# Which DRAM run each SBUF partition takes: K and V pieces read in an interleaved order

## The chip, the cores and the metric

The kernel runs on one core of one Trainium2 chip. The metric is device time in microseconds (us) of one execution. The time before is 656.44 us, the median of three executions (656.38 to 656.63).

## What is computed

One decode step of a transformer block for a single token: layer norm, grouped-query attention over a cached context of 65,536 tokens, a residual, a second layer norm, a gated MLP and a second residual. All inputs are bf16.

```python
# x (1,1,512); k_cache, v_cache (1,8,65536,128); wq (512,4096); wo (4096,512)
q = layernorm(x) @ wq                      # 32 query heads of 128, four to each of the 8 KV heads
p = softmax(q . k_cache * 128**-0.5)       # over the 65,536 cached tokens
h = x + (p . v_cache) @ wo
g, u = layernorm(h) @ w_gate, layernorm(h) @ w_up      # 512 -> 1792
out = h + (sigmoid(g) * u) @ w_down
```

The two caches are 134 MB each; all weights together are some 14 MB. A softmax over tokens and the sum over V don't depend on the order in which the tokens are visited, as long as K and V use the same order.

## The kernel before, in words

**Pieces.** The work goes head by head, `h` = 0 to 7. The 65,536 tokens of a head of K, and of V, come in two *pieces* of 32,768 tokens, 8 MiB each (`PIECES`, line 229). A piece is spread over the 128 SBUF partitions: partition p holds 256 consecutive tokens, that is one DRAM *run* of 256 x 128 bf16 = 64 KiB. Within a partition a piece is 16 *chunks* of 16 tokens (`TC`), 4 KiB each. So a piece is 128 runs of 64 KiB, one for each partition, and the piece is contiguous in DRAM.

**The ring.** K and V pieces land in one SBUF tile, `ring`, with room for 36 chunks (line 230). `AT` (line 231) says where: the two K pieces of a head at chunks 0 and 4 (they overlap), both V pieces at chunk 20. Only the first head's K and the last head's V get two places apart, 0 and 20.

**Loads.** `load` (lines 325 to 331) issues one DMA for one piece, or for some columns (`cols`) of one. All are issued on SP's queue, in the order of the program: two loads of `wq`; K of head 0 in four parts of 8 chunks (lines 336 to 339); then for each head h = 1 to 7 the four pieces K h.0, V h-1.0, K h.1, V h-1.1 (lines 340 to 344); V 7.0; most of `wo`; V 7.1 in two parts (10 and 6 chunks, `LAST`); the rest of `wo`; and the weights of the MLP (lines 345 to 367). Each issue waits on SP until its place in the ring is free: a K piece waits for a mark F on VectorE, set when 12 of the 16 chunks of the K piece before it have been transposed (lines 526 to 528; `ORDER`, line 232, visits chunks 4 to 15 of the first piece first, so that the overlapping next piece can come in). A V piece waits for the matmuls that read the V piece before it (PV, line 599). SP does nothing else.

**Compute.** VectorE transposes each chunk of K in 32 x 32 blocks into `ktw` (line 525), TensorE forms the scores of four query heads from it (`pe_scores`, line 536; all matmuls with register addresses are recorded at line 436), VectorE and ScalarE form the softmax of the head (line 554), VectorE transposes the probabilities into `PT_sb` (line 581), and TensorE sums V with them (`pv`, line 599) while the next head's K comes in. The last head's sum is followed by `wo`, the second layer norm and the MLP (lines 822 to 880).

**What the step of the change touches.** Line 329 cuts the DRAM side of a piece into 128 rows, one for each partition; line 331 issues the DMA with that and the ring's columns. Every K and V load goes through these two lines: 18 of K and 17 of V. The weights have lines of their own.

Of the kernel before, what the change touches and what calls it, by code (L numbers as in the profile page):

```python
# [20 lines left out]
TC = 16  # L21
# [14 lines left out]
class Prog:  # L36
# [20 lines left out]
    def dma(self, eng, fn, sem, deps=(), name=None):  # L57
        self.op(eng, fn, deps, name)
        rec = self.dma_sems.setdefault(sem, dict(sem=None, count=0))
        rec["count"] += 16  # L60
        self.ops[eng][-1]["dma"] = (sem, rec["count"])
# [155 lines left out]
def bass_sequential_preLN__gqa_block_cached__glu_gated_glu__decode_kernel(  # L217
# [10 lines left out]
    CH = TC * DH  # L228
# [11 lines left out]
    with ExitStack() as es:  # L240
        def sb(name, shape, dt):
            return es.enter_context(nc.sbuf_tensor(name, shape, dt))
# [14 lines left out]
        ring = sb("ring", [128, RING], bf16)  # L257
# [57 lines left out]
        op, dma = P.op, P.dma  # L315
# [6 lines left out]
        def first_chunk(k, h, q):  # L322
            return AT[{("K", 0): "K0", ("V", HKV - 1): "V7"}.get((k, h), k)][q]

        def load(k, h, q, deps, sem, name, cols=None):
            j0, j1 = PIECES[q]
            a, z = cols or (j0, j1)
            cache = A_k_cache if k == "K" else A_v_cache
            rows = cache[0, h, j0 * TC * 128:j1 * TC * 128, :].rearrange("(p t) d -> p (t d)", p=128)
            at = (first_chunk(k, h, q) - j0) * CH  # L330
            dma("sp", lambda e: e.dma_start(ring[:, at + a * CH:at + z * CH], rows[:, (a - j0) * CH:(z - j0) * CH]), sem, deps, name)  # L331

        wq_rows = A_wq.rearrange("(p k) n -> p (k n)", p=128)
        for nm, a, z in (("wq0", 0, NQ * DH), ("wq", NQ * DH, NKT * CH)):
# [1 line left out]
        for q in range(2):  # L336
            for i in range(2):
                j0 = 16 * q + 8 * i
                load("K", 0, q, (), f"r{2 * q + i + 1}", f"K0.{q}{'ab'[i]}", (j0, j0 + 8))
        for h in range(1, HKV):  # L340
            load("K", h, 0, ["F0.0" if h == 1 else f"F{h - 1}.1"], "ka", f"K{h}.0")
            load("V", h - 1, 0, ["F0.1" if h == 1 else f"PV{h - 2}.3"], "va", f"V{h - 1}.0")
            load("K", h, 1, [f"F{h}.0"], "kb", f"K{h}.1")
            load("V", h - 1, 1, [f"PV{h - 1}.1"], "vb", f"V{h - 1}.1")
        h = HKV - 1
# [11 lines left out]
        for k, w in (("wg", B_w_gate), ("wu", B_w_up)):  # L357
            src = w.rearrange("(p k) n -> p (k n)", p=128)
            for i, (k0, k1) in enumerate(W_SPLIT[k]):
                at = W_AT[k]  # L360
# [3 lines left out]
        for i, (r0, r1) in enumerate(WD_SPLIT):  # L364
            at = AT["wd"] * CH
# [470 lines left out]
        for i, (nm, bank) in enumerate((("wg", GB), ("wu", UB))):  # L836
            at = W_AT[nm]
# [73 lines left out]
```

## Time and profile before

| | |
|---|---|
| time, median of three | 656.44 us (656.38 to 656.63) |
| time of the profiled execution | 656.46 us |
| its span, first to last instruction | 655.1 us |
| around the span | 1.4 us |
| HBM read | 282.33 MB |
| VectorE busy | 350.4 us (53%) |
| TensorE busy (matmul) | 401.2 us (61%) |
| ScalarE, GpSimd busy | 43.1 us, 3.7 us |
| mean granted TensorE clock | 0.774 |

The span is what the hardware profiler records between the first and the last instruction. "Busy" counts instructions that compute; the issuing of a DMA isn't counted. Matmuls are pipelined, so a busy TensorE isn't one at its peak. In the rows below, names such as `ring<-in_A_k_cache_dram` are a transfer's destination and source, and an `SPq` row is the issue of a DMA on SP. The chain of waits is followed back from the last instruction, at each step to what released it.

### The profile page before, as it was taken

How to read it: one execution, taken by the hardware profiler on the slowest of the kernel's cores; microseconds unless marked ns; L12 is line 12 of the kernel's file. 1: busy time of each engine (PE TensorE's matmuls, PEld its weight loads, DVE VectorE, ACT ScalarE, POOL GpSimd, SP SyncE). 2: the span in 40 equal slices, each digit the busy share in tenths (PEclk: the TensorE clock that was granted, in tenths of full speed). 3: DMA queues.
4: the chain of work that ended last, by engine and by line, in shares of the span. 5: the costliest groups of instructions: out<-in, count | busy, mean ns of one | idle time of the engine just before them, and what ended most of it. 6: DMA issues, size and time to landing. Idle time of an engine off the chain costs nothing.

```text
span 655.1 us, 6177 instructions
## 1 busy us (share of the span) xinstructions
PE 401.2 (61%) x2317; PEld 67.0 (10%) x1549; DVE 350.4 (53%) x428; ACT 43.1 (7%) x114; POOL 3.7 (1%) x19
## 2 busy tenths in 40 slices
PE   2678672938548283774828567392855839285476
PEld 1100010110101000010100101010010101001122
DVE  3498953819366290935719184481917548092202
ACT  1100200020000200002000200002000020001101
POOL 1000000000000000000000000000000000000000
PEclk9899695966959598685978769596885959778655
DMA  9999989998999999998999999999999989999998
GB/s 414 418 448 448 448 384 448 448 448 384 448 448 448 420 412 448 448 448 384 448 448 448 428 404 448 448 448 396 436 448 448 448 384 448 448 448 416 423 413 366
DMA packets 6517, 282.35 MB, mean 431 GB/s; under 512 B 754, under 2 KB 884, under 8 KB 1268
## 3 DMA queue, kind: packets, MB, share of 16 engines
q1 hardware_dynamic: 6484, 282.33, 99.7%
q8 instruction: 1, 0.02, 0.0%
q10 hardware_dynamic: 32, 0.00, 0.0%
HBM read 282.33 MB, written 0.00 MB: 431 GB/s over the span
## 4 chain that ended last, share of the span: by engine, by line
DMA 66%; DVE 30%; PE 2%; issue 1%; SPq 0%; PEldq 0%
DMA ring<-in_A_k_cache_dram 58%; DVE ktw L525 30%; DMA ring<-in_B_w_up_dram 4%; DMA ring<-in_A_v_cache_dram 4%; PE PS L436 2%; PE PS L860 0%; PE PS L841 0%; DVE hh L853 0%; DVE hhT L857 0%; SPq L361 0%; SPq L331 0%; DVE y_sb L878 0%; PEldq L171 0%
## 5 line engine op out<-in xcount | busy, mean ns | idle before, releaser
L525 DVE STREAM_TRANSPOSE ktw<-ring 128x1024 f32<-128x1024 f32 x256 | 291.7, 1208 | 164.7 <-DMA ring<-in_A_k_cache_dram 164.6
L436 PE MATMUL PS<-ktw 128*128 128x512 bf16 x1024 | 276.8, 420 | 162.1 <-DVE ktw L525 154.7
L436 PE MATMUL PS<-ring,PT_sb 128*32 x1024 | 88.0, 434 | 53.1 <-issue 45.2
L436 PEld LDWEIGHTS PS<-ktw 128*128 x256 | 26.2, 103 | 401.2 <-issue 233.7
L612 ACT ACTIVATE po_sb<-PS,rl 128x512 bf16<-128x512 f32 x8 | 5.5, 687 | 524.0 <-PE PS L436 524.0
L436 PEld LDWEIGHTS PS<-ring,PT_sb 128*32 x1024 | 20.7, 116 | 117.7 <-issue 116.3
L560 DVE TENSOR_REDUCE gmj<-PS 1x4 f32<-1x128 f32 x8 | 2.2, 279 | 54.3 <-PE PS L558 54.3
L532 DVE TENSOR_REDUCE M_sb<-PS 128x1 f32<-128x512 f32 x32 | 19.9, 683 | 19.3 <-PE PS L436 19.3
L571 ACT ACTIVATE P_sb<-PS,negmax 128x512 bf16<-128x512 f32 x32 | 21.5, 685 | 0.3
L581 DVE STREAM_TRANSPOSE PT_sb<-P_sb 128x512 bf16<-128x512 bf16 x32 | 19.8, 674 | 1.7 <-ACT P_sb L571 1.7
L436 PE MATMUL PS<-ktw,xz 128*8 x32 | 9.4, 467 | 2.5 <-DMA ktw<-in_A_wq_dram 2.5
L628 DVE TENSOR_TENSOR Lw<-O,blk_of 128x896 bf16<-128x896 bf16 (+1 forms) x2 | 1.4, 683 | 16.0 <-ACT O L618 16.0
L565 PE MATMUL PS<-one_f,gmrep 1*128 1x1 f32 x16 | 4.6, 357 | 5.0 <-DVE gmrep L562 5.0
L558 PE MATMUL PS<-identf,gm 128*1 128x128 f32 x16 | 4.5, 379 | 5.0 <-issue 2.9
L637 DVE CAST O<-PS 128x28 bf16<-128x28 f32 (+1 forms) x2 | 0.3, 174 | 12.7 <-PE PS L634 12.7
L483 DVE STREAM_TRANSPOSE qt<-qh 32x512 bf16<-32x512 bf16 x1 | 0.7, 699 | 11.1 <-ACT qh L480 11.1
L571 ACT ACTIVATION_READ_ACCUMULATOR P_sb<-PS,negmax 128x1 f32 x32 | 6.5, 202 | 0.0
L615 PE MATMUL PS<-sel_bf,po_sb 128*128 128x4 bf16 x32 | 2.1, 171 | 6.3 <-ACT po_sb L612 6.3
L416 PE MATMUL PS<-xs,xpick 16*128 16x32 bf16 x1 | 0.2, 202 | 8.3 <-DMA xs<-in_A_x_dram 8.3
L498 ACT ACTIVATE PS<-zcol 128x512 f32<-128x512 bf16 x8 | 5.0, 622 | 0.0
L567 ACT ACTIVATE negmax<-PS 128x1 f32<-128x1 f32 x8 | 1.4, 171 | 54.1 <-PE PS L565 54.1
L586 PE MATMUL PS<-L_sb,lsel 128*128 128x4 f32 x16 | 2.5, 229 | 3.8 <-DVE PT_sb L581 3.8
(90 smaller groups left out, 69.7 us busy)
## 6 DMA issues: line engine op xcount, KB each, us to landing
ring<-in_A_k_cache_dram SPq DMA_DIRECT2D x4, 4096.0 KB, 34.2
ring<-in_A_v_cache_dram SPq DMA_DIRECT2D x1, 5120.0 KB, 30.1
ktw<-in_A_wo_dram SPq DMA_DIRECT2D x1, 3584.0 KB, 18.4
ktw<-in_A_wq_dram SPq DMA_DIRECT2D x1, 3072.0 KB, 11.5
ring<-in_A_v_cache_dram SPq DMA_DIRECT2D x1, 3072.0 KB, 36.9
ring<-in_B_w_gate_dram SPq DMA_DIRECT2D x1, 1792.0 KB, 23.8
ring<-in_B_w_up_dram SPq DMA_DIRECT2D x1, 1792.0 KB, 27.7
ktw<-in_A_wq_dram SPq DMA_DIRECT2D x1, 1024.0 KB, 4.6
```

The source lines that it names most:

```text
L436: return e.add_instruction(mybir.InstMatmult(name=nc.get_next_instruction_name(), engine=mybir.EngineType.PE, ins=[rhs, lhsT], outs=[e.low ...
L498: op("act", lambda e: e.activation(ps(PO, 0, 512), bass.AP(tensor=zcol, offset=0, ap=[[1, 128], [0, 512]]), AF.Copy), ["zcol"] if h == 0 e ...
L525: op("dve", lambda e, d=dst, sr=src: e.transpose(d, sr), deps, f"T{b}.{c}", to="T")
L532: op("dve", lambda e, u=u: e.tensor_reduce(M_sb[:, u % 4:u % 4 + 1], ps(u % NS, 0, 512), AX.X, ALU.max), [f"S{b}.{NC - NR + k}"], f"mx{u}" ...
L558: op("pe", lambda e: e.matmul(ps(MISC, 0, 128, 0, 1), lhsT=gm[:, :], rhs=identf[:, :], start=True, stop=True), [f"gm{h}"], f"gmT{h}", to="Q")
L560: op("dve", lambda e: e.tensor_reduce(gmj[:, :], ps(MISC, 0, 128, 0, 1).rearrange("p (i a c) -> p a i c", a=4, c=NC), AX.XY, ALU.max), [f" ...
L565: op("pe", lambda e: e.matmul(ps(MISC, 128, 129), lhsT=gmrep[0:1, :], rhs=one_f[0:1, 0:1], start=True, stop=True), [f"gmrep{h}"], f"neg{h}")
L571: op("act", lambda e, b=b: e.activation(P_sb[:, (b % 4) * 512:(b % 4 + 1) * 512], ps(b % NS, 0, 512), AF.Exp, bias=negmax[:, k:k + 1], sca ...
L581: op("dve", lambda e, b=b: e.transpose(PT_sb[:, (b % 4) * 512:(b % 4 + 1) * 512], P_sb[:, (b % 4) * 512:(b % 4 + 1) * 512]), [f"E{b}"], f" ...
L586: op("pe", lambda e: e.matmul(ps(MISC, 132, 136), lhsT=lsel[:, :], rhs=L_sb[:, :], start=True, stop=True), [f"PT{NR * h + NR - 1}"], f"l{h ...
L612: op("act", lambda e: e.activation(po_sb[:, :], ps(PO, 0, 512), AF.Copy, scale=rl[:, :]), [f"PV{h}.{NR - 1}", f"rl{h}"], f"po{h}", to="po")
L615: op("pe", lambda e, t=t: e.matmul(ps(OX, 0, 4), lhsT=po_sb[:, t * 128:(t + 1) * 128], rhs=sel_bf[:, 8 * t:8 * t + 8:2], start=(t == 0), s ...
```

## The change

The 128 runs of a piece are handed to the partitions in another order. Write a partition's number as 8e + j, with e from 0 to 15 and j from 0 to 7. Before, partition 8e + j took run 8e + j of the piece. After, it takes run 16j + e. So the eight partitions 8e to 8e + 7 took eight runs that follow each other in DRAM, and now take eight runs that are 16 runs (1 MiB) apart; at one j, the sixteen values of e make up one contiguous MiB.

```diff
             cache = A_k_cache if k == "K" else A_v_cache
-            rows = cache[0, h, j0 * TC * 128:j1 * TC * 128, :].rearrange("(p t) d -> p (t d)", p=128)
+
+            rows = cache[0, h, j0 * TC * 128:j1 * TC * 128, :].rearrange("(j e t) d -> e j (t d)", j=8, e=16)
             at = (first_chunk(k, h, q) - j0) * CH
-            dma("sp", lambda e: e.dma_start(ring[:, at + a * CH:at + z * CH], rows[:, (a - j0) * CH:(z - j0) * CH]), sem, deps, name)
+            dma("sp", lambda e: e.dma_start(ring[:, at + a * CH:at + z * CH], rows[:, :, (a - j0) * CH:(z - j0) * CH]), sem, deps, name)
```

In the program that is built, the DRAM side of these 35 DMAs changes from two dimensions, 128 x 32,768 elements, to three, 16 x 8 x 32,768 (steps of 64 KiB, 1 MiB and one element; fewer elements where a load takes some of the columns). The SBUF side is written 128 x 1 x 32,768 instead of 128 x 32,768 and names the same bytes in the same order. The order of the instructions on every engine, their waits and all other DMAs are unchanged; one blank line more moves the line numbers after it by one. K and V are permuted alike.

## The prediction

> **What bounds the kernel now.** First the page: busy times, the row of DMA shares, the queues.
>
> ```profile
> span 655.1 us, 6177 instructions
> ...
> PE 401.2 (61%) x2317; PEld 67.0 (10%) x1549; DVE 350.4 (53%) x428; ACT 43.1 (7%) x114; POOL 3.7 (1%) x19
> ...
> DMA  9999989998999999998999999999999989999998
> GB/s 414 418 448 448 448 384 448 448 448 384 448 448 448 420 412 448 448 448 384 448 448 448 428 404 448 448 448 396 436 448 448 448 384 448 448 448 416 423 413 366
> DMA packets 6517, 282.35 MB, mean 431 GB/s; under 512 B 754, under 2 KB 884, under 8 KB 1268
> ...
> q1 hardware_dynamic: 6484, 282.33, 99.7%
> ```
>
> No compute engine is busy for more than 61% of the span, but SP's queue (q1) keeps the 16 DMA engines at work for 99.7% of it. The GB/s row runs flat at 448 with a 384 now and then; whole packets are booked into slices, so their mean of 431 is what counts. There is no room between transfers: the kernel ends when 282 MB are in.
>
> Next the chain of waits, in order of time.
>
> ```profile
> 1.66 29.59 DMA ring<-in_A_k_cache_dram
> ...
> 44.96 25.00 DMA ring<-in_A_k_cache_dram
> ...
> 83.77 25.14 DMA ring<-in_A_k_cache_dram
> ...
> 161.55 24.76 DMA ring<-in_A_k_cache_dram
> 186.33 13.67 DVE ktw L525 x13
> 200.02 24.98 DMA ring<-in_A_k_cache_dram
> ...
> 238.70 24.88 DMA ring<-in_A_k_cache_dram
> ...
> 547.93 24.75 DMA ring<-in_A_k_cache_dram
> 572.71 13.67 DVE ktw L525 x13
> 586.39 24.96 DMA ring<-in_A_v_cache_dram
> ...
> 621.26 27.67 DMA ring<-in_B_w_up_dram
> ```
>
> The chain looks like a loop of two parts: a K piece lands, VectorE transposes 13 chunks (13.67 us), that frees the ring for the next K piece, which lands 24.9 us after its issue. I read it otherwise. From 186.31 (161.55 + 24.76) to 572.68 (547.93 + 24.75) there are ten loops in 386.37 us, 38.64 us each. In each loop one K and one V piece come in, so a piece takes 38.64 / 2 = **19.32 us** of the DMA engines: 8.39 MB / 19.32 us = 434 GB/s. Of the 24.9 us between issue and landing, 24.9 - 19.3 = 5.6 us are a wait behind the V piece that was issued before. That 5.6 us is all the slack between the loop through VectorE and the engines' own pace.
>
> Last, whether the ceiling belongs to the caches or to the way in. The stretches by window (us, then the busy times, DMA share and GB/s last):
>
> ```profile
> 31.00:70.00 39.00, 29.23 (x123) 3.37 (x33) 34.85 (x39) 0.23 (x2) 0.00 (x0) 0.98 1.03 444
> ...
> 187.00:225.00 38.00, 23.68 (x136) 3.79 (x88) 20.65 (x25) 4.68 (x13) 0.00 (x0) 0.77 1.02 442
> ...
> 612.00:649.00 37.00, 25.14 (x215) 7.43 (x219) 2.57 (x14) 1.17 (x3) 0.55 (x1) 0.55 0.99 426
> ```
>
> The stretch from 612 to 649 us moves the last V piece (10 and 6 chunks of 4 KiB in two parts), the rest of `wo` and the MLP's weights, so runs of 40 KiB and less, at 426 GB/s; pure K and V with runs of 64 KiB come at 442. Sources and distances in DRAM differ, the rate hardly does. So I take the ceiling to be the 16 engines and their way into SBUF, 434 / 16 = 27.1 GB/s each, and not the DRAM.
>
> **The change part by part.**
>
> *Instructions.* The order of the instructions is the same on all five engines and nothing is added. The 35 issues of K and V have a DRAM side with one dimension more. What an issue costs on SP now:
>
> ```profile
> L331 SPq DMA_DIRECT2D ring<-in_A_k_cache_dram x18: 327/328/477, 1.3 to 547.9; - x18
> ```
>
> 0.33 us. If the third dimension doubled that, a K piece would be issued 0.33 us later, inside the slack of 5.6 us: zero. Without that cover it would be 35 x 0.33 = 11.5 us.
>
> *Compute.* Which token sits in which partition changes, no shape does: zero.
>
> *Transfers.* Bytes and run lengths stay (128 runs of 64 KiB), so the packets should. Two things change: which DRAM addresses are read at the same time, and which engine writes which partition. [...] No bulk transfer of this form is in the trace, so the cost is bounded.
>
> - Lower bound: every engine keeps its own way into SBUF and a piece takes its 19.32 us. It cannot take less by much: the quickest loop is 263.58 - 225.00 = 38.58 us (landings of the rows at 238.70 and 200.02), the mean over 14 loops from 31.25 (1.66 + 29.59) to 572.68 is 38.67, so all loops at the quickest pace save 14 x 0.09 = 1.3 us.
> - Upper bound: the way in is shared by two engines at a time while others lie idle, so a piece takes 2 x 19.32 = 38.64 us. Two is the smallest whole number of engines that can meet.
>
> I take the **upper bound**. The resource has 0.3% to spare, so a collision there shows at its full price; the rows put the ceiling on the engines' side, where the hand-out now changes; and as all engines start a piece together with equal packets, two that meet on their first run meet on all.
>
> [...]
>
> *Sum.* 32 pieces are 16 pairs, 16 x 38.64 = 618.2 us of the span. Everything else (`wq`, `wo`, the MLP's weights, start and end) keeps its form: 655.1 - 618.2 = 36.9 us. Doubled: 618.2 + 618.2 + 36.9 = 1273.3, with the 1.4 us around the span 1274.7. The profiled execution (656.46) is 0.02 us above the median, so no correction: **1275 us**. No second bound appears: by the compute on the loop, 13.67 + 38.64 = 52.3 us, against 77.3 us of transfers.
>
> **The rivals.**
>
> 1. *Not slower: the hand-out doesn't matter.* Place: the way into SBUF. [...] Price: nothing, at best -1.3 us: 655.2 to 657.5 us. It decides where no two engines meet, wherever their partitions lie. For it: the trace shows no shared way. The 1.3 us are 0.2% of 656, about what a measurement of this kernel can tell from no change, so a gain beyond that needs a ceiling higher than any stretch shows.
> 2. *Engines meet, but fall out of step.* If pairs that meet drift apart, or one of a pair is served first, only part of the time is doubled. With 0.2 of it shared: 656.5 + 0.2 x 618.2 = 780 us; with 0.8: 1151 us. For it: loops differ by up to 0.37 us now (38.95 for the landing at 108.91, 38.58 for the quickest), and SP is one piece ahead, so a leading engine may run on. [...] A DRAM that serves the new order worse ends in this span too: at two thirds of the rate, 656.5 + 618.2 / 2 = 966 us.
> [...]
>
> [...]
>
> **How the numbers follow.** Forecast, doubled: 0.66, with its own range of 1240 to 1290 (a twentieth of the added 618 lost to drift, or 15 us for dearer sharing). Rival 1: 0.11, of which 0.02 faster by over 0.2% and 0.09 within it. Rival 2: 0.15. Rival 3: 0.05. Above 1290: 0.03. Slower by over 0.2%: 0.66 + 0.15 + 0.05 + 0.03 = 0.89. The range takes the forecast and rival 2, from 780 to 1290, together 0.81.
>
> **What the profile after would show.** Right: the mean GB/s near 282 / 1273 = 222, the engines' share still near 99% (packets last longer, none is missing), K landings 77.3 us apart, and a K piece landing 77.3 - 13.7 = 63.6 us after its issue. Compute busy times stay, their shares halve. The weights at the end, in their old form, still come at some 430 GB/s: the sharpest sign that the form is the cause. Rival 1: loops of 38.6 us as now. Rival 2: loops of uneven length, the first ones perhaps slower than the later. [...] Engines' share well below 99% would mean that generating or issuing the longer pattern is the limit, which I hold at nothing. I am wrong from the ground up if the packets become shorter: then the count of 6517 changes.

## The result and the profile after

The changed kernel takes 1328.65 us (median of 6, 1308.88 to 1334.14) against 656.54 us before in the same runs: a ratio of 2.010, with a 95% interval of 1.996 to 2.024. Three of the six executions (1329.12, 1331.37 and 1334.14 us) count as slow ones, and the ratio is that of the means of the fast ones, 1320.35 over 656.85 us. The forecast was a doubling, 1275 us; the time lies 54 us above it and 39 us above the end of the range. The kind of slowdown is the one that was forecast, packets that last about twice as long, its size is not; that two engines share a way into SBUF no run shows.

The page of the changed kernel: span, the shares of the DMA engines and GB/s in 40 slices, packets, the queue.

```profile
span 1326.8 us, 6177 instructions
...
DMA  9999999999999999999999999999999999999998
GB/s 272 218 205 221 190 221 215 196 221 190 221 194 217 219 192 221 190 221 194 217 219 192 221 190 221 202 209 221 190 221 190 221 202 209 221 190 221 190 269 277
DMA packets 6517, 282.35 MB, mean 213 GB/s; under 512 B 754, under 2 KB 884, under 8 KB 1268
...
q1 hardware_dynamic: 6484, 282.33, 100.0%
```

The same 6517 packets and the same bytes; the 16 engines are never idle, yet they move 213 GB/s in place of 431. No transfer was added and no gap opened: each packet (one run, moved by one engine) lasts longer.

The landings of K, seen from VectorE (start, length, what, and in brackets the idle time before and what ended it):

```profile
213.09 14.93 DVE L526 STREAM_TRANSPOSE ktw<-ring 128x1024 f32<-128x1024 f32 x13 [58.90 <-DMA ring<-in_A_k_cache_dram]
...
293.82 14.81 DVE L526 STREAM_TRANSPOSE ktw<-ring 128x1024 f32<-128x1024 f32 x13 [28.29 <-DMA ring<-in_A_k_cache_dram]
...
374.56 14.94 DVE L526 STREAM_TRANSPOSE ktw<-ring 128x1024 f32<-128x1024 f32 x13 [59.01 <-DMA ring<-in_A_k_cache_dram]
```

A K piece lands every 80.74 us, (374.56 - 213.09) / 2; it was 38.64, and 77.3 was forecast. What the issues say (median us from issue to landing, then the length of one issue):

```profile
ring<-in_A_v_cache_dram SPq DMA_DIRECT2D x15, 71.2
ring<-in_A_k_cache_dram SPq DMA_DIRECT2D x14, 66.9
```

```profile
L332 SPq DMA_DIRECT2D ring<-in_A_k_cache_dram x18: 536/537/638, 1.3 to 1115.0; - x18
```

An issue takes 0.54 us in place of 0.33, and hides. And the end, by window (DMA share and GB/s last), in which the MLP's weights come in their old form:

```profile
200.00:400.00 200.00, 68.03 (x330) 8.64 (x186) 63.27 (x71) 4.68 (x13) 0.00 (x0) 0.64 1.01 210
...
1310.00:1320.00 10.00, 5.73 (x63) 2.03 (x63) 1.70 (x12) 0.86 (x2) 0.33 (x1) 0.67 1.02 417
```

The same engines in the same run carry weights at 417 GB/s and K and V at 210. So the slowness belongs to the changed transfers and not to the run. The trace's packet records say more than any view. They name no engine and no partition, but where one packet's end meets the next one's start they fall into sixteen sequences, one for each engine. Here is the median length in us of the 64 KiB packets, by place in each engine's fours (first and fifth, second and sixth, and so on, of a piece's eight).

```
                    1st    2nd    3rd    4th
before              2.42   2.42   2.42   2.42
after               4.89   5.10   5.11   5.12
```

Four long packets, the first a little shorter, and again: the lengths repeat every four packets, that is every four runs. Each engine's share of a transfer ends with a packet of 4 bytes, and by these all sixteen engines stay in step: they end their shares of a piece within 1 us of one another in every piece, at 30.6 to 31.5 us as at 1260.9 to 1261.8 us.

### The profile page after: what moved, and what is told of

The parts are those of the page before. It is cut to its first block, busy times and chain, and to the rows that moved or that the text cites. A ratio compares the mean times of both kernels' runs of the same rounds, so it can differ in the third digit from the quotient of the medians.

```text
span 1326.8 us, 6177 instructions
## 1 busy us (share of the span) xinstructions
PE 432.3 (33%) x2317; PEld 65.6 (5%) x1549; DVE 350.8 (26%) x428; ACT 43.1 (3%) x114; POOL 3.7 (0%) x19
## 2 busy tenths in 40 slices
DMA packets 6517, 282.35 MB, mean 213 GB/s; under 512 B 754, under 2 KB 884, under 8 KB 1268
## 5 line engine op out<-in xcount | busy, mean ns | idle before, releaser
L437 PE MATMUL PS<-ktw 128*128 128x512 bf16 x1024 | 284.4, 427 | 502.4 <-DVE ktw L526 502.1
L437 PE MATMUL PS<-ring,PT_sb 128*32 x1024 | 112.0, 542 | 352.4 <-PEq L171 317.4
L566 PEld LDWEIGHTS PS<-one_f,gmrep 1*128 1x128 f32 x16 | 3.8, 291 | 8.7 <-DVE gmrep L563 8.7
L437 PE MATMUL PS<-ktw,O 128*1 x28 | 3.9, 586 | 0.7 <-DVE O L638 0.7
```

Source lines behind the costliest of these rows:

```text
L437: return e.add_instruction(mybir.InstMatmult(name=nc.get_next_instruction_name(), engine=mybir.EngineType.PE, ins=[rhs, lhsT], outs=[e.low ...
L566: op("pe", lambda e: e.matmul(ps(MISC, 128, 129), lhsT=gmrep[0:1, :], rhs=one_f[0:1, 0:1], start=True, stop=True), [f"gmrep{h}"], f"neg{h}")
```

## The experiments

Theories: **hand-out** (what counts is which partitions are written at the same time: with 16 rows outermost, or with all engines on 64 partitions, the engines hold each other up, with 32 or 128 rows they don't; that they do so in pairs, on one way into SBUF, was my assumption), **reading order** (the interleaved DRAM addresses are slow) and **form** (three dimensions are slow in themselves).

**near16: the new hand-out with the old reading order.**

```diff
-rows = cache[0, h, j0 * TC * 128:j1 * TC * 128, :].rearrange("(j e t) d -> e j (t d)", j=8, e=16)
+rows = cache[0, h].rearrange("(e q j t) d -> q e j (t d)", e=16, q=2, j=8)[q]
```

Partition 8e + j of piece q takes run 16e + 8q + j of the head's 256. By the hand-out theory this stays slow.

> [...] Reading-order theory (the interleaved DRAM order is what is slow): back to 656. Form theory (a DRAM pattern of three dimensions is slow in itself): 1328.

Measured: 1328.56 us, ratio 2.023 (2.020 to 2.026). Slow without interleaving, and with all of the further 54 us: neither the doubling nor the excess comes from the reading order. Its page has the packets and the rate of the changed kernel:

```profile
DMA packets 6516, 282.33 MB, mean 212 GB/s; under 512 B 754, under 2 KB 884, under 8 KB 1268
...
q1 hardware_dynamic: 6484, 282.33, 100.0%
```

**near32: three dimensions, 32 rows outermost** (`e=32, q=2, j=4` in the same line).

By the hand-out theory this is as fast as before.

> The same with 32 rows outermost (partition 4e + j of piece q takes run 8e + 4q + j of the head): three dimensions, DRAM order nearly as before. [...] Reading-order theory: 656. Form theory: 1328.

Measured: 656.26 us, ratio 0.9999 (0.999 to 1.001). The form theory falls. The dearer issue is there and hidden:

```profile
L332 SPq DMA_DIRECT2D ring<-in_A_k_cache_dram x18: 534/535/619, 1.3 to 547.7; - x18
```

**rows32: a still wider interleaving, 32 rows outermost.**

```diff
-.rearrange("(j e t) d -> e j (t d)", j=8, e=16)
+.rearrange("(j e t) d -> e j (t d)", j=4, e=32)
```

Partition 4e + j takes run 32j + e.

> [...] Hand-out theory: 656 us within 0.3%. Reading-order theory: slow, 1200 to 1400. Form theory: 1328.

Measured: 656.37 us, ratio 1.000 (0.999 to 1.001). The window of its loop has the 442 GB/s of before:

```profile
187.00:225.00 38.00, 22.77 (x136) 3.73 (x88) 20.61 (x26) 4.68 (x13) 0.00 (x0) 0.81 1.02 442
```

The reading-order theory falls: neighbouring runs on partitions four apart, and 2 MiB between the runs of neighbouring partitions in each four, cost nothing here.

**half64: the old form in two halves.**

```diff
-dma("sp", lambda e: e.dma_start(ring[:, lo:hi], rows[:, ...]), sem, deps, name)
+for g in range(2):      # partitions 64g to 64g + 63; the semaphore counts go to 32
+    dma("sp", lambda e, ...: e.dma_start(ring[p0:p1, lo:hi], rows[p0:p1, ...]), sem, ...)
```

By the hand-out theory this is slow.

> The kernel before, each K and V load issued as two DMAs, partitions 0 to 63 and 64 to 127; two dimensions on both sides, DRAM order as before. [...] Reading-order and form theories: 656 to 660.

Measured: 1335.13 us, ratio 2.034 (2.031 to 2.037). From its page:

```profile
DMA packets 7077, 282.34 MB, mean 212 GB/s; under 512 B 1314, under 2 KB 1444, under 8 KB 1828
...
q1 hardware_dynamic: 7044, 282.34, 100.0%
```

Old order, old dimensions, all engines busy, and as slow. What is new is that 16 engines work on 64 partitions at a time; that a load is two DMAs isn't the cause by itself, for eng8 below makes it four and its packets keep 2.42 us. Why 64 partitions at a time are slow for 16 engines no run shows.

**eng8: eight rows outermost, four partitions each.**

```diff
+rows = cache[0, h].rearrange("(g e q j t) d -> q g e j (t d)", g=4, e=8, q=2, j=4)[q]
+for g in range(4): dma(... ring[32 * g:32 * g + 32, lo:hi] <- rows[g] ...)     # the semaphore counts go to 64
```

If the rows are dealt one to an engine, eight engines work, and if these don't hold each other up, the loop doubles by that alone.

> Each K and V load issued as four DMAs of 32 partitions with a DRAM side of 8 x 4 runs (partition 32g + 4e + j of piece q takes run 64g + 8e + 4q + j of the head). [...] If all sixteen engines work: 656. Form theory: 1328 or more.

Measured: 1282.37 us, ratio 1.953 (1.949 to 1.956). Its page and its landings of K:

```profile
DMA  6445444544454455445444544454445445545674
GB/s 278 213 213 229 213 213 213 229 213 213 213 229 213 213 225 217 213 213 229 213 213 213 227 215 213 213 227 215 213 213 229 213 213 219 223 213 227 251 269 194
```

```profile
205.54 14.81 DVE L528 STREAM_TRANSPOSE ktw<-ring 128x1024 f32<-128x1024 f32 x13 [55.67 <-DMA ring<-in_A_k_cache_dram]
...
360.14 14.81 DVE L528 STREAM_TRANSPOSE ktw<-ring 128x1024 f32<-128x1024 f32 x13 [55.45 <-DMA ring<-in_A_k_cache_dram]
```

Half of the engines are idle (tenths of 4 and 5), and the loop takes (360.14 - 205.54) / 2 = 77.30 us, the forecast doubling; its packets last 2.42 us. So eight engines at 2.42 us a packet are faster than sixteen at 4.89 to 5.12, and the difference, 80.74 - 77.30 = 3.44 us a loop, 55 us in 16 loops, is what the changed kernel pays beyond a doubling. (The 7 us that eng8 has beyond 1275 lie outside these loops and were not followed.)

**heads4: the change for heads 0 to 3 alone** (`j=8 if h < 4 else 1, e=16 if h < 4 else 128` in the rearrangement).

> The change for heads 0 to 3 alone, K and V alike; heads 4 to 7 as before. If each changed piece pays for itself and nothing carries over: half of the added 672 us, so 992 us, with loops of some 82 us in the first half and of 38.6 in the second of one profile. If a piece of the old form beside a changed one, or the state that the changed ones leave, costs too: more than 1000.

Measured: 995.22 us, ratio 1.515 (1.513 to 1.518). Both kinds of loop in one run:

```profile
60.00:600.00 540.00, 179.17 (x906) 23.80 (x540) 155.71 (x178) 17.38 (x49) 0.00 (x0) 0.65 1.00 216
700.00:960.00 260.00, 155.51 (x936) 24.74 (x640) 131.38 (x153) 18.36 (x51) 0.00 (x0) 0.76 1.00 435
```

Each piece pays for itself: 995.22 us is 3 us from the 992 of that theory, and the old rate is back in the second half.

**stagger, lag2, lag4: putting the engines out of step.** If engines hold each other up because they are in step, a lag between them should undo it. Two DMAs from DRAM to a spare place in DRAM, which do no part of the computation, put 12 engines and then four behind: by four packets each in stagger and lag4, which is the period of the packet lengths above, and by two in lag2.

```diff
+for n in (12, 4):       # stagger: ahead of K 0; lag2, lag4: behind the first V piece
+    spare = nc.dram_tensor(f"spare{n}", [n, r + 1, TC * CH], bf16, kind="Internal").ap()
+    src = ...           # part of V of the last head, cut into rows in the same way
+    dma("sp", lambda e, ...: e.dma_start(spare[:, 0:r], src[:, 0:r]), f"lag{n}", ...)   # r packets of 64 KiB on n engines
```

> [...] Reading-order and form theories: 1328 plus 10 to 20.

Measured: 1329.70 us, ratio 2.025 (2.022 to 2.028): not the 800 to 1000 us that I had put on engines out of step, and by itself what the other two theories gave. The packet records show why the lag didn't help. K of head 0 comes in runs of 32 KiB, so four packets of 64 KiB are eight of these, a whole load: engines with one lag and with none were in step again, one load apart, while the four with both ran half a load behind. From 80 to 87 us the four without a lag had no work, and just then the 32 KiB packets of the other twelve mostly took 1.21 us, in place of some 2.53 before. From the next pieces to the end the engines ran in groups one and two packets apart (shares of one piece end at 324, 330 and 341 us), at the slow rate.

> [...] If engines don't meet, or if being in step doesn't matter: 1335.

> [...] The engines ahead run out of issued work when they lead by more than the queue does, so the lag can't keep in full; hand-out theory: 800 to 1000 us, less than with two packets. Otherwise 1340.

Measured: lag2 1335.70 us, ratio 2.034 (2.031 to 2.037), and lag4 1311.44 us, ratio 1.999 (1.996 to 2.002): lag2's is the 1335 us of no gain, and lag4's, far above its forecast, shows nothing by itself, as one execution of the changed kernel took 1308.88. But lag4 has a stretch that settles it (windows of lag4; the pieces right behind the lag are in the second line):

```profile
120.00:170.00 50.00, 17.88 (x66) 2.04 (x18) 21.00 (x23) 0.00 (x0) 0.00 (x0) 0.67 1.02 210
...
185.00:209.00 24.00, 0.00 (x0) 0.00 (x0) 0.00 (x0) 0.00 (x0) 0.00 (x0) 0.50 1.03 434
211.00:228.00 17.00, 10.50 (x37) 1.04 (x10) 14.02 (x14) 0.00 (x0) 0.00 (x0) 0.70 0.56 239
235.00:290.00 55.00, 18.44 (x105) 3.03 (x81) 15.95 (x20) 4.68 (x13) 0.00 (x0) 0.60 1.00 209
```

The changed kernel's own DMAs run at 434 GB/s, the old ceiling, as long as the lag lasts (up to 193 us four engines still carry packets of the lag, but from 193 to 213 us all is K and V, and it is 429). Then the engines ahead run out of issued work (share 0.56 from 211 us; the next K piece is issued at 227.67 us). Twelve engines start that piece together and four follow about a packet behind (shares end at 308.7 to 309.8 and at 313.9 to 316.1 us, and so on to the end), at 209 GB/s for the rest. I had expected more of the lag to stay.

**only4, only8, only12: which engines meet.** lag2 gained nothing even at first (218 GB/s from 185 to 209 us). So the lag of four packets was put on 4, 8 or 12 engines. By my assumption of pairs, set against set of four engines, a lag on 4 or on 12 parts two of the four sets and leaves the other two in step, and a lag on 8 parts none.

```diff
-for n in (12, 4) if h == 1 else ():
+for n in (4,) if h == 1 else ():        # (8,) and (12,) in the other two
```

> [...] What is read is the rate of the two pieces that follow, between some 195 and 220 us. Pairs that pay each for themselves: half of the engines at full rate, 310 to 330 GB/s, packets of 2.4 and of 5.1 us side by side. One meeting pair holds up all sixteen (which would explain why two packets of lag gained nothing): 200 to 215 GB/s, no packets of 2.4 us beyond the lag's own.

> [...] Hand-out theory: the two pieces behind the lag run at the slow rate, some 205 GB/s, once all engines are at work. If it is enough that the engines are spread in time, whatever they write: some 430 GB/s as with both lags.

> [...] Pairs that pay each for themselves: 310 to 330 GB/s behind the lag; one meeting pair holds up all: 200 to 215.

Measured, one execution each: 1343.49, 1344.09 and 1338.03 us. The same 24 us as above, in only4, then only8, then only12 (a packet counts whole where it starts, so 218 in this window is the slow rate of some 210):

```profile
185.00:209.00 24.00, 0.00 (x0) 0.00 (x0) 0.00 (x0) 0.00 (x0) 0.00 (x0) 0.51 1.06 218
```

```profile
185.00:209.00 24.00, 0.00 (x0) 0.00 (x0) 0.00 (x0) 0.00 (x0) 0.00 (x0) 0.50 1.06 218
```

```profile
185.00:209.00 24.00, 0.00 (x0) 0.00 (x0) 0.00 (x0) 0.00 (x0) 0.00 (x0) 0.50 1.05 218
```

All slow, where both lags together gave 434. In only12 the four engines without a lag ran a full four packets ahead (shares end at 202 and 222 us), and still the packets of the pieces behind the lag were long. In only4 and only8 the four packets of lag came to two packets of some 5 us (shares end at 213 and 222 us in only4, 212 and 222 in only8). So a spread in time isn't enough, with 4, 8 or 12 engines behind; of these lags only the two together brought the old rate back.

In the packet records of only4, while four engines were still at their lag's packets (DRAM to DRAM, 2.42 us each but for the first), all of the other twelve took 4.88 to 5.13 us a packet, though the four weren't writing to SBUF at all. If pairs paid each for themselves and the four had their partners among the twelve, as assumed, four of the twelve would have been at 2.42 us. So what held up some of the twelve held up all; how few engines would do it, no run shows. The lag of lag2 lasted to the end, with groups one and two packets apart (shares end at 206, 216 and 221 us); why that gained nothing is not shown. No run shows an engine's number either, nor which partitions an engine writes.

## Why the prediction was wrong, step by step

- *What bounds the kernel* (the engines' way into SBUF, 19.32 us a piece, not the DRAM): right that it isn't the DRAM. near32 and rows32 change the reading order at 656.3 and 656.4 us, half64 keeps it at 1335. Whether an engine alone is held by its way into SBUF or by itself stays open: the lag's packets, which don't go to SBUF, take the same 2.42 us. No run shows that a way into SBUF is the limit. Shown is that with 16 rows outermost the engines in step take up to 5.12 us a packet, and that the same DMAs ran at 434 GB/s in lag4's stretch.
- *Instructions at zero*: right. Issues went from 0.33 to 0.54 us, and near32 shows them hidden.
- *Transfers, two engines on one way, 2 x 19.32 us a piece*: that engines hold each other up fits near16, half64 and lag4. But no run shows two engines on one way, the factor in the sum, nor which partitions an engine writes before and after. What the runs show in its place is a packet of 4.89 to 5.12 us for 2.42. The doubling was taken as an **upper bound**, with nothing in the sum beyond it, and there it failed. eng8 measures a doubling by half of the engines at 77.30 us a loop, the changed kernel 80.74. A packet takes up to 5.12 us, not 2 x 2.42 = 4.84, so some 6% more. Why is open. With the measured loop the sum is 16 x 80.74 + 36.9 + 1.4 = 1330.1 us, for 1328.65.
- *The range*: its end of 1290 left 15 us for dearer sharing, with no row behind the figure; 55 came on top of the doubling. The lower end, 780, came from rival 2, which the packet records of the changed kernel rule out (below).
- *Not slower* (rival 1) and *out of step* (rival 2, and rival 3 with its 0.05): fell. In the profiled execution of the changed kernel all engines stay in step to the end (the one of 1308.88 us has no profile, and what made it shorter is open). Of the lags that were put in, five gained nothing (stagger, lag2, only4, only8, only12), and the one that gained emptied the queue and was mostly gone after two pieces (lag4). The two thirds of the DRAM's rate fell with rows32.
- *Signs*: engines' share (100.0%), packet count (6517) and the weights' rate at the end (417 GB/s) came close to what was named; 213 GB/s in place of 222, and 66.9 us to landing in place of 63.6, are the same excess again.

## What to carry to other kernels

In these runs the shape of a DMA's DRAM side decided the rate: 128 runs of 64 KiB into the same 128 partitions made the kernel 656 us with 32 or 128 rows outermost and 1329 with 16. When a transfer-bound kernel slows down with the engines 100% busy and the packets unchanged in number, look at the length of a packet and at the rows outermost before the DRAM addresses. And a doubling was no upper bound here: 55 us came on top.

## What the runs showed of the hardware that was not expected

- Sixteen engines in step pay more than a doubling: up to 5.12 us for a 64 KiB packet, against 2.42 in eng8, so two engines carry 25.6 GB/s (2 x 64 KiB in 5.12 us) where one alone carries 27.1. Why is open.
- With four engines away at DRAM-to-DRAM packets, which keep 2.42 us, the other twelve, which write to SBUF, still take 4.88 to 5.13 us a packet (only4). What couples them is open.
- Eight engines can beat sixteen: 1282.37 us against 1328.65.
- A lag between engines that gained nothing lasted for the whole run (lag2: shares of one piece end at 1211, 1221 and 1226 us). The one that gained lasted for two pieces, until the engines ahead had no work left (lag4).
